# v of the retention stage moved from SyncE's issue queue to ScalarE's

## The chip, the cores and the metric

The kernel runs on one core of one Trainium2 chip. TensorE (PE) does the matrix products, VectorE (DVE) and ScalarE (ACT) the elementwise work, GpSimd (POOL) a little of it, and SyncE (SP) issues transfers. Any of these engines has a queue of instructions that it takes strictly in order; a transfer (DMA) is an instruction in the queue of the engine that issues it, and the data is then moved by 16 DMA engines that all queues share. The metric is device time in microseconds (us), lower is better.

## The reference, cut to what matters

Three parts run one after the other: retention over 8 heads, then two feed-forward layers.

```python
q, k, v: (2 batches, 8 heads, 768 positions, 64), float32; lam: (8,)
for each block of 64 positions:
    intra = (q_b @ k_b.T * Dmask) @ v_b          # Dmask[i, j] = lam ** (i - j) for i >= j
    inter = (q_b * lam ** (pos + 1)) @ kv_state
    out_b = intra + inter
    kv_state = lam ** 64 * kv_state + (k_b * lam ** (63 - pos)).T @ v_b
x = out as (1536 tokens, 512)
h = x @ w_in;  x = (h * tanh(softplus(h))) @ w_out          # layer 1, w_in 512 x 2048
h = x @ w_in2; x = where(h > 0, h, exp(h) - 1) @ w_out2     # layer 2
```

## The kernel before, in words

**Retention** (`retention`, L126) takes the 768 positions of each batch in 6 chunks of 128, 12 chunks in all, numbered 0 to 11, batch by batch in turn. For a chunk it needs three inputs of 256 KB each, called kn, qn and vn by the profile (k3 below is kn of chunk 3, and so on). A loop over rounds n = 0 to 13 (L368) overlaps the chunks. In round n, in this order:

- transfers: k and q of chunk n + 3, v of chunk n + 1, and from round 5 on a weight tile (`raw`, 512 KB, at most two in a round);
- `second_part` of chunk n - 2 on DVE: xl, the low part of x (out of PSUM, minus xh), which frees the single PSUM buffer `o`; the running state `sd`;
- `scores` of chunk n on PE (tile sc, L275), `decay` on DVE (am, L283);
- `transposes` of chunk n + 1 on PE (tile Tp, L231), copied to SBUF by one ACT instruction (tile T, L237). `scores` of the next round reads T;
- `scaled_q` on DVE, `block_state` of chunk n - 2 on ACT (sbd, L350, two instructions);
- `outputs` of chunk n - 1 on PE (o, L305, which reads vn; then st, L314), and `first_part` on ACT: xh, the high part of x (L325);
- `scaled_k` on POOL (kd, L255).

`pin` holds all of these in the order in which they are written. kn, qn and vn have four buffers each (`io`, `bufs=4`), so k of chunk n + 3 is loaded where k of chunk n - 1 was.

All transfers stand in SP's queue, except lam (4 KB), which ACT issues at the start. The framework gives every transfer one of eight completion counters, in turn, in the order in which it plans them; the instruction that issues a transfer first waits until the last holder of its counter has landed, that is, the transfer eight places earlier in that order. The listings of instructions name these counters DMAHW0 to DMAHW7.

**The two layers** follow (`unit`, L518): x is held as a high and a low part (xh, xl) and the weights likewise, so that each product is three matmuls in a fast float32 form. The weights come in 64 tiles of 512 KB which DVE and ACT split (`w_steps`, L86). The first units of layer 1 are interleaved with the end of retention.

Of the kernel before, what the change touches and what calls it, by code (L numbers as in the profile page):

```python
# [18 lines left out]
def kernel(  # L19
# [12 lines left out]
    nc = tc.nc  # L32
# [93 lines left out]
    def retention(beside_load, beside_step, at_end):  # L126
# [12 lines left out]
        def pin(ins):  # L139
            tc.keep_in_program_order(ins)  # L140
            return ins

        def load(n, names, parts=1):
            if not 0 <= n < NC:
                return
            b, c = chunks[n]
            for nm in names:
                nat[n, nm] = io.tile([P, H, D], F32, tag=nm + "n", name=nm + "n")
            for y in range(parts):
                for nm in names:  # L150
                    src, t = {"k": k, "q": q, "v": v}[nm], nat[n, nm]
                    hs = slice(y * H // parts, (y + 1) * H // parts)
                    pin(nc.sync.dma_start(  # L153
                        out=t[:, hs],
                        in_=src[b, hs, c * P:(c + 1) * P, :].rearrange("h p d -> p h d"),
                    ))
# [3 lines left out]
        nc.scalar.dma_start(out=lam_b.rearrange("p h o -> p (h o)"), in_=lam.partition_broadcast(P))  # L160
        load(1, "kq")
        load(2, "kq")
        load(0, "v")

        idle = cst.tile([P, P], F32, name="idle")
        pin(nc.vector.memset(idle, 0.0))
# [5 lines left out]
        def powers(m, end):  # L172
            if m == 1:
                for hh in range(2):
                    rows = slice(hh * D, (hh + 1) * D)
                    pin(nc.vector.tensor_copy(
                        lq[rows, :, 0:1], lam_b[rows].rearrange("p (r t) o -> p r t o", t=2)[:, :, hh]
                    ))
            while m < end:
                pin(nc.vector.tensor_tensor(  # L180
                    out=lq[:, :, m:2 * m], in0=lq[:, :, 0:m],
                    in1=lq[:, :, m - 1:m].to_broadcast([P, PR, m]), op=ALU.mult,
                ))
                m *= 2
# [27 lines left out]
        def warm(count):  # L212
            ps = psO.tile([P, PR, P], F32, tag="o", name="warm")
            for _ in range(count):
                pin(nc.tensor.matmul(ps[:, 0], lhsT=idle, rhs=idle, start=True, stop=True))

        def transposes(n, parts=1):

            T2 = P // 2
            both = wk.tile([P, 2, PR, P], F32, tag="T", name="T")  # L220
            ps = psT.tile([P, 2, 2, PR, T2], F32, tag="T", name="Tp")
            for y in range(parts):
                if y > 0:
                    warm(2)
                rs = slice(y * PR // parts, (y + 1) * PR // parts)
                for z, nm in enumerate(("k", "q")):
                    x = nat[n, nm]
                    for r in range(rs.start, rs.stop):
                        for h in range(2):
                            rows = slice(h * T2, (h + 1) * T2)  # L230
                            pin(nc.tensor.transpose(  # L231
                                ps[:, h, z, r],
                                x[rows, 2 * r:2 * r + 2].rearrange("p h d -> p (h d)"),
                                ident[rows, rows],
                            ))
                if parts == 1:
                    pin(nc.scalar.activation(  # L237
                        out=both.rearrange("p z r (h t) -> p h (z r) t", h=2),
                        in_=ps.rearrange("p h z r t -> p h (z r) t"), func=AF.Copy,
                    ))  # L240
                else:
                    for z in range(2):
                        pin(nc.scalar.activation(
                            out=both[:, z, rs].rearrange("p r (h t) -> p h r t", h=2),
                            in_=ps[:, :, z, rs], func=AF.Copy,
                        ))
            tr[n] = both[:, 0], both[:, 1], ps

        def scaled_k(n):
            if n >= NC:  # L250
                return
            kd = None
            if chunks[n][1] < NCH - 1:
                kd = wk.tile([P, H, D], F32, tag="kd", name="kd", bufs=3)
                pin(nc.gpsimd.tensor_tensor(  # L255
                    out=kd, in0=nat[n, "k"], in1=dm[:, :, P - 1:P].to_broadcast([P, H, D]), op=ALU.mult
                ))
            kds[n] = kd

        def scaled_q(n):  # L260
            if n < NC and chunks[n][1] > 0:
                q2 = wk.tile([P, PR, P], F32, tag="q2", name="q2", bufs=3)
                pin(nc.vector.tensor_tensor(  # L263
                    out=q2.rearrange("p r (h t) -> p h r t", h=2), in0=tr[n][2][:, :, 1],
                    in1=lq.rearrange("p r (h t) -> p h r t", h=2), op=ALU.mult,
                ))
                q2s[n] = q2

        def scores(n):
            kT, qT, _ = tr[n]  # L270
            ps = psS.tile([P, 2, PR, P], F32, tag="sc", name="sc")
            for r in range(PR):
                for hh in range(2):
                    rows = slice(hh * D, (hh + 1) * D)
                    last = pin(nc.tensor.matmul(  # L275
                        ps[:, hh, r], lhsT=kT[rows, r], rhs=qT[rows, r], start=True, stop=True
                    ))
            sc[n] = ps
            return last

        def decay(n):
            a = wk.tile([P, 2, PR, P], F32, tag="am", name="am")
            pin(nc.vector.tensor_tensor(  # L283
                out=a, in0=sc.pop(n), in1=dm.rearrange("p (r t) i -> p t r i", t=2), op=ALU.mult
            ))
            am[n] = a
# [34 lines left out]
        def first_part(n):  # L321
            o, st = done[n]
            b, c = chunks[n]
            t, col = divmod(n * P, TB)
            pin(nc.scalar.activation(out=xh[t][:, :, col:col + P], in_=o, func=AF.Copy))  # L325
            if st is not None and c > 0:
                pin(nc.gpsimd.tensor_tensor(out=sd[b], in0=sd[b], in1=lc, op=ALU.mult))

        def second_part(n):
            o, st = done[n]  # L330
            b, c = chunks[n]
            t, col = divmod(n * P, TB)
            pin(nc.vector.tensor_tensor(  # L333
                out=xl[t][:, :, col:col + P],
                in0=o,
                in1=xh[t][:, :, col:col + P].bitcast(F32),
                op=ALU.subtract,
            ))
            if st is not None:
                if c > 0:  # L340
                    pin(nc.vector.tensor_tensor(out=sd[b], in0=sd[b], in1=st, op=ALU.add))
                else:
                    pin(nc.vector.tensor_copy(sd[b], st))
# [11 lines left out]
        def warm_tiles(count):  # L355

            ps = [psO.tile([P, PR, x], F32, tag=t, name="warm") for t, x in (("o", P), ("st", D))]
            for x in range(count):
                y, z = divmod(x % 4, 2)
                rows, cols = slice(y * D, (y + 1) * D), slice(z * D, (z + 1) * D)  # L360
                pin(nc.tensor.matmul(
                    ps[y][cols, 0, 0:D], lhsT=idle[rows, 0:D], rhs=idle[rows, 0:D], start=True, stop=True
                ))

        warm(7)
        transposes(0, 2)
        warm_tiles(24)
        for n in range(NC + 2):  # L368
            load(n + 3, "kq")
            load(n + 1, "v")  # L370
            beside_load(n, pin)
            if n >= 2:
                second_part(n - 2)
                beside_step(n, 0, pin)
            if n < NC:
                last = scores(n)
                decay(n)
            if n == 1:
                powers(8, P)
            if n + 1 < NC:  # L380
                transposes(n + 1)
            if n == 0:
                warm(2)
                scaled_k(0)
            if n + 1 < NC:
                scaled_q(n + 1)
            if n >= 2:
                block_state(n - 2)
            if 0 < n <= NC:
                outputs(n - 1)  # L390
                first_part(n - 1)
            scaled_k(n + 1)
            beside_step(n, 1, pin)
        with tc.issue_after(last.ins):
# [161 lines left out]
    def beside_load(n, pin):  # L556
        for m in LOAD.get(n, ()):
            pin(w_load(m))

    def beside_step(n, place, pin):  # L560
        for _ in range(STEPS.get((n, place), 0)):
            pin(next(todo))
# [52 lines left out]
```

## Time and profile before

| | |
|---|---|
| median of 3 runs (lowest, highest) | 584.43 us (584.27, 587.32) |
| profiled execution: its own time | 584.7 us |
| profiled execution: span, first to last instruction | 582.4 us |
| PE busy over the span | 574.4 us (99%) |
| DVE, ACT, POOL busy | 430.9, 231.5, 18.9 us |
| granted TensorE clock, mean | 0.999 |
| transfers: kn, qn, vn | 11 each of kn and qn at 256 KB and 4 halves, 12 of vn |
| median issue to landing of vn, kn, qn (256 KB) | 5.2, 5.2, 5.0 us |

The profiled execution's time is 2.3 us longer than its span (start and end of the program lie around it). A row of the timeline gives the start, the length, the engine, the source line and the tiles, and in brackets how long that engine stood idle before it and what ended the idle time. Retention takes about the first 62 us; its last outputs (chunk 11) start at 59.8 us.

### The profile page before, as it was taken

Reading aid. Unit: us, or ns where it says so; the run is one execution under the profiler, and the core shown is the slowest. Engines: PE = TensorE matmul, PEld = TensorE weight load, DVE = VectorE, ACT = ScalarE, POOL = GpSimd, SP = SyncE. Lnnn points to the kernel's source line nnn. Section 1 sums busy time; section 2 is a strip of 40 time slices with the busy share of each in tenths; the row PEclk is TensorE's granted clock in tenths of the full one; section 3 lists DMA queues with packets and bytes.
Section 4 is the critical chain, followed back from the end, with each engine's and each line's share of the span. In section 5 each row is a group of like instructions: output and inputs, shape, how many; then the busy total and the mean of one; then the engine's idle time right before and its main releaser. Section 6 shows DMA issues by size and latency. Waiting matters only on the chain.

```text
span 582.4 us, 8221 instructions
## 1 busy us (share of the span) xinstructions
PE 574.4 (99%) x3282; PEld 481.2 (83%) x3282; DVE 430.9 (74%) x798; ACT 231.5 (40%) x390; POOL 18.9 (3%) x28
## 2 busy tenths in 40 slices
PE   7999999999999999999999999999999999999997
PEld 6988888888888888888888888888888888888886
DVE  5769999998399726993599956995499957944342
ACT  3655554344134124233346445555145235235220
POOL 4430000000000000000000000000000000000000
PEclk9999999999999999999999999999999999999999
DMA  9998333334023301322022221321022310000112
GB/s 172 214 219 233 109 110 108 110 111 142 0 74 108 109 1 37 106 79 69 1 72 73 73 73 36 110 74 71 1 73 72 109 36 1 1 1 0 73 54 92
DMA packets 61030, 46.67 MB, mean 80 GB/s; under 512 B 38848, under 2 KB 55488, under 8 KB 60992
## 3 DMA queue, kind: packets, MB, share of 16 engines
q1 hardware_dynamic: 60848, 46.14, 28.2%
q8 instruction: 26, 0.43, 0.3%
q14 instruction: 12, 0.10, 0.1%
q10 hardware_dynamic: 144, 0.00, 0.0%
HBM read 43.00 MB, written 3.15 MB: 79 GB/s over the span
## 4 chain that ended last, share of the span: by engine, by line
PE 93%; DMA 2%; DVE 2%; SPq 1%; ACT 1%; issue 1%; ACTq 0%
PE h L423 44%; PE y L465 43%; PE o L305 2%; PE y L480 2%; DMA qn<-in_q_dram 1%; DMA vn<-in_v_dram 1%; SPq L153 1%; PE sc L275 1%; PE Tp L231 1%; PE st L314 0%; DVE xl L333 0%; DVE b L104 0%; DVE u L111 0%; DVE q L263 0%; ACT xh L325 0%
## 5 line engine op out<-in xcount | busy, mean ns | idle before, releaser
L423 PE MATMUL h<-xh,w 128*128 128x512 f32 x768 | 240.7, 389 | 0.1
L423 PEld LDWEIGHTS h<-xh,w 128*128 128x128 f32 x768 | 144.1, 188 | 30.5 <-ACT w L118 0.6
L423 PE MATMUL h<-xl,w 128*128 128x512 f32 x384 | 149.4, 389 | 0.0
L465 PE MATMUL y<-w,g 128*128 128x512 f32 (+1 forms) x588 | 132.5, 385 | 0.0
L465 PEld LDWEIGHTS y<-w,g 128*128 128x128 f32 x588 | 108.9, 188 | 22.1
L465 PE MATMUL y<-g,w 128*128 128x512 f32 x528 | 121.5, 389 | 0.0
L465 PEld LDWEIGHTS y<-g,w 128*128 128x128 f32 x528 | 99.1, 188 | 20.6
L493 DVE TENSOR_TENSOR acc<-acc,y 128x512 f32<-128x512 f32 (+1 forms) x73 | 49.4, 677 | 58.6 <-PE y L465 58.6
L433 DVE TENSOR_TENSOR g<-g,g 128x512 fp32r<-128x512 f32 x96 | 65.9, 687 | 30.0 <-ACT g L432 27.5
L423 PEld LDWEIGHTS h<-xl,w 128*128 128x128 f32 x384 | 72.1, 188 | 14.9
L118 ACT ACTIVATE w<-m 128x512 fp32r<-128x512 f32 x64 | 40.2, 628 | 102.0 <-PE h L423 55.2
L432 ACT ACTIVATE g<-g 128x512 fp32r<-128x512 f32 x96 | 60.2, 628 | 16.3 <-DVE g L450 14.8
L119 DVE TENSOR_TENSOR w<-m,w 128x512 fp32r<-128x512 f32 x64 | 43.9, 686 | 24.4 <-ACT w L118 23.7
L441 ACT ACTIVATE g<-h 128x512 f32<-128x512 f32 x48 | 28.5, 596 | 71.1 <-PE h L423 71.1
L447 ACT ACTIVATE e<-h 128x512 f32<-128x512 f32 x48 | 28.6, 596 | 59.0 <-PE h L423 58.0
L450 DVE SCALAR_TENSOR_TENSOR g<-e,h 128x512 f32<-128x512 f32 x48 | 32.8, 683 | 17.1 <-ACT e L448 17.0
L104 DVE SCALAR_TENSOR_TENSOR b<-raw,b 128x512 int32<-128x512 int32 x64 | 44.1, 690 | 0.4
L111 DVE SCALAR_TENSOR_TENSOR u<-raw,u 128x512 f32<-128x512 uint32 x64 | 43.7, 684 | 0.2
L116 DVE TENSOR_TENSOR m<-b,u 128x512 f32<-128x512 f32 x64 | 43.7, 684 | 0.1
L448 ACT ACTIVATE e<-e 128x512 f32<-128x512 f32 x48 | 30.3, 631 | 1.1
L98 DVE TENSOR_SCALAR m<-m 128x512 f32<-128x512 f32 x64 | 27.1, 424 | 0.1
L107 DVE TENSOR_SCALAR u<-b 128x512 int32<-128x512 int32 x64 | 26.8, 420 | 0.4
(52 smaller groups left out, 304.3 us busy)
## 6 DMA issues: line engine op xcount, KB each, us to landing
raw<-in_moe_w_in_dram SPq DMA_DIRECT2D x32, 512.0 KB, 3.7
raw<-in_moe_w_out_dram SPq DMA_DIRECT2D x32, 512.0 KB, 3.3
vn<-in_v_dram SPq DMA_DIRECT2D x12, 256.0 KB, 5.2
kn<-in_k_dram SPq DMA_DIRECT2D x11, 256.0 KB, 5.2
qn<-in_q_dram SPq DMA_DIRECT2D x11, 256.0 KB, 5.0
out_dram<-acc SPq DMA_DIRECT2D x11, 256.0 KB, 2.0
kn<-in_k_dram SPq DMA_DIRECT2D x2, 128.0 KB, 3.5
qn<-in_q_dram SPq DMA_DIRECT2D x2, 128.0 KB, 3.6
```

Source lines behind the costliest of these rows:

```text
L104: yield nc.vector.scalar_tensor_tensor(out=b, in0=hw, scalar=-0x40000000, in1=b, op0=ALU.bitwise_and, op1=ALU.bitwise_or)
L111: yield nc.vector.scalar_tensor_tensor(out=uf, in0=lw, scalar=2.0 ** -52, in1=uf, op0=ALU.mult, op1=ALU.mult)
L116: yield nc.vector.tensor_tensor(out=mf, in0=bf, in1=uf, op=ALU.add)
L118: nc.scalar.activation(out=w[:, 0], in_=mf, func=AF.Copy)
L119: yield nc.vector.tensor_tensor(out=w[:, 1], in0=mf, in1=w[:, 0].bitcast(F32), op=ALU.subtract)
L423: nc.tensor.matmul(h, lhsT=lt, rhs=rt, start=(kk == 0 and n == 0), stop=(kk == KD - 1 and n == 2),)
L432: nc.scalar.activation(out=gg[:, 0], in_=g, func=AF.Copy)
L433: nc.vector.tensor_tensor(out=gg[:, 1], in0=g, in1=gg[:, 0].bitcast(F32), op=ALU.subtract)
L448: nc.scalar.activation(out=e, in_=e, func=AF.Exp, scale=-1.0)
L450: nc.vector.scalar_tensor_tensor(out=g, in0=e, scalar=-1.0, in1=h, op0=ALU.add, op1=ALU.max)
L465: nc.tensor.matmul(y, lhsT=lt, rhs=rt, start=(i == 0 and n == 0), stop=(i == G - 1 and n == 2),)
L493: nc.vector.tensor_tensor(out=dst, in0=dst, in1=y, op=ALU.add)
```

## The change

v of every chunk is issued by ACT instead of SP, and at another place in the round: v0 behind the copies of the transposes of chunk 0, v1 in round 0 behind the copy of the transposes of chunk 1, and v of chunk n + 2 at the end of round n, behind xh of chunk n - 1. Nothing is computed otherwise.

```diff
-                    pin(nc.sync.dma_start(
+                    pin((nc.scalar if nm == "v" else nc.sync).dma_start(
...
         load(1, "kq")
         load(2, "kq")
-        load(0, "v")
...
         transposes(0, 2)
+        load(0, "v")
         warm_tiles(24)
         for n in range(NC + 2):
             load(n + 3, "kq")
-            load(n + 1, "v")
...
             if n == 0:
+                load(1, "v")
                 warm(2)
                 scaled_k(0)
...
                 outputs(n - 1)
                 first_part(n - 1)
+            load(n + 2, "v")
             scaled_k(n + 1)
```

On PE, DVE and POOL the instructions stand as before. ACT's queue in the middle of retention, before: the copy T of chunk 7, sbd of chunk 4, xh of chunk 5, the copy T of chunk 8.

```order
L237 ACTIVATE T<-Tp 128x2x8x64 [waits PE_49,Activation_49]
L350 ACTIVATE sbd_139<-sd_137 64x4x64 [waits DVE_49,Activation_49]
L350 ACTIVATE sbd_139<-sd_137 64x4x64 [waits Activation_49]
L325 ACTIVATE xh_65<-o 128x4x128 [waits PE_49]
L237 ACTIVATE T<-Tp 128x2x8x64 [waits PE_49,Activation_49]
```

The same stretch of ACT's queue in the changed kernel:

```order
L236 ACTIVATE T<-Tp 128x2x8x64 [waits PE_49,Activation_49]
L349 ACTIVATE sbd_137<-sd_135 64x4x64 [waits DVE_49,Activation_49]
L349 ACTIVATE sbd_137<-sd_135 64x4x64 [waits Activation_49]
L324 ACTIVATE xh_65<-o 128x4x128 [waits PE_49]
L153 DMA vn<-in_v_dram 128x8x64 [waits DMAHW7_49]
L236 ACTIVATE T<-Tp 128x2x8x64 [waits PE_49,Activation_49]
```

Between xh of chunk 5 and the copy T of chunk 8 the issue of v8 now stands, with a wait for counter 7. SP's queue before, from the first weight tile on: raw0, k9, q9, v7, k10, q10, v8, k11.

```order
L75 DMA raw<-in_moe_w_in_dram 128x4x256 [waits DMAHW4_49]
L153 DMA kn<-in_k_dram 128x8x64 [waits DMAHW5_49,PE_49,Pool_49]
L153 DMA qn<-in_q_dram 128x8x64 [waits DMAHW6_49,PE_49]
L153 DMA vn<-in_v_dram 128x8x64 [waits DMAHW7_49,PE_49]
L153 DMA kn<-in_k_dram 128x8x64 [waits DMAHW0_49,PE_49,Pool_49]
L153 DMA qn<-in_q_dram 128x8x64 [waits DMAHW1_49,PE_49]
L153 DMA vn<-in_v_dram 128x8x64 [waits DMAHW2_49,PE_49]
L153 DMA kn<-in_k_dram 128x8x64 [waits DMAHW3_49,PE_49,Pool_49]
```

SP's queue in the changed kernel from the same weight tile on: raw0, k9, q9, k10, q10, k11, q11, raw1.

```order
L75 DMA raw<-in_moe_w_in_dram 128x4x256 [waits DMAHW2_49]
L153 DMA kn<-in_k_dram 128x8x64 [waits DMAHW4_49,PE_49,Pool_49]
L153 DMA qn<-in_q_dram 128x8x64 [waits DMAHW7_49,DMAHW5_49,PE_49]
L153 DMA kn<-in_k_dram 128x8x64 [waits DMAHW7_49,PE_49,Pool_49]
L153 DMA qn<-in_q_dram 128x8x64 [waits DMAHW3_49,DMAHW0_49,PE_49]
L153 DMA kn<-in_k_dram 128x8x64 [waits DMAHW2_49,PE_49,Pool_49]
L153 DMA qn<-in_q_dram 128x8x64 [waits DMAHW6_49,DMAHW3_49,PE_49]
L75 DMA raw<-in_moe_w_in_dram 128x4x256 [waits DMAHW4_49]
```

The v's are gone from it. The counters of both queues together are dealt in this order in the changed kernel (the planner places a v among SP's transfers by when it expects ACT to come to it; a and b are the halves of chunk 0):

```
counter   0    1    2     3    4    5    6    7
         lam  k0a  q0a   k0b  q0b  k1   q1   k2
         q2   k3   q3    v0   k4   q4   k5   q5
         v1   v2   k6    q6   v3   k7   q7   v4
         k8   q8   raw0  v5   k9   q9   v6   k10
         q10  v7   k11   q11  raw1 raw2 raw3 v8
         v9   v10  v11
```

Each transfer waits for the one above it: v1 for q2, v2 for k3, v3 for k4, v4 for q5, v8 for k10.

## Rows read from the trace of the kernel before

**Rows 1.** Busy time by engine: retention and rest (us, count; PEclk, DMA share, GB/s)

```profile
0.00:62.00 62.00, 57.26 (x991) 52.66 (x991) 47.51 (x79) 31.41 (x53) 18.89 (x28) 1.00 0.92 201
62.00:582.40 520.40, 517.17 (x2292) 428.54 (x2292) 383.36 (x720) 200.06 (x338) 0.00 (x0) 1.00 0.21 66
sum 582.40, PE 574.43 PEld 481.19 DVE 430.87 ACT 231.48 POOL 18.89; mean PE 287.21 PEld 240.60 DVE 215.44 ACT 115.74 POOL 9.44
```

**Rows 2.** Waits of PE in 0 to 62 us (us in total, times, longest)

```profile
PE o L305 <- DMA vn<-in_v_dram: 1.5, 1, 1.5
PE Tp L231 <- DMA qn<-in_q_dram: 1.2, 2, 1.0
...
PE sc L275 <- ACT T L237: 0.5, 1, 0.5
```

**Rows 3.** Busy time in three stretches of 2 us; last columns DMA share, GB/s

```profile
8.00:10.00 2.00, 1.52 (x28) 1.27 (x26) 1.23 (x1) 1.02 (x1) 1.96 (x2) 1.00 1.32 224
...
12.00:14.00 2.00, 0.94 (x18) 0.97 (x20) 1.79 (x6) 0.72 (x1) 0.00 (x0) 1.00 0.71 159
14.00:16.00 2.00, 2.00 (x52) 1.93 (x47) 1.49 (x4) 0.60 (x1) 1.06 (x1) 1.00 1.11 239
```

**Rows 4.** Timeline of SP's queue: issue of q9, v7, k10 (start, length)

```profile
33.52 0.89 SPq L153 DMA_DIRECT2D qn<-in_q_dram  x1
34.50 2.33 SPq L153 DMA_DIRECT2D vn<-in_v_dram  x1
36.94 1.62 SPq L153 DMA_DIRECT2D kn<-in_k_dram  x1
```

**Rows 5.** Issues starting at 2.89, 5.67, 6.75, 17.05, 36.94: last column us to landing

```profile
kn<-in_k_dram SPq DMA_DIRECT2D x1, 256.0 KB, 4.2
...
qn<-in_q_dram SPq DMA_DIRECT2D x1, 256.0 KB, 5.0
...
vn<-in_v_dram SPq DMA_DIRECT2D x1, 256.0 KB, 6.2
...
qn<-in_q_dram SPq DMA_DIRECT2D x1, 256.0 KB, 6.0
...
kn<-in_k_dram SPq DMA_DIRECT2D x1, 256.0 KB, 5.3
```

**Rows 6.** Timeline of ACT: its one transfer, then the round of xh of chunk 5

```profile
0.74 0.43 ACTq L160 DMA_DIRECT2D lam_b<-in_lam_dram  x1
1.20 1.28 ACT L168 ACT_TABLE_LOAD   x1 [1.20 <-PEq L597]
...
33.49 0.60 ACT L325 ACTIVATE xh<-o 128x512 fp32r<-128x512 f32 x1
35.53 1.03 ACT L237 ACTIVATE T<-Tp 128x1024 f32<-128x1024 f32 x1 [1.45 <-PE Tp L231]
36.58 0.86 ACT L350 ACTIVATE sbd<-sd 64x256 f32<-64x256 f32 x2
```

**Rows 7.** Tile vn: issues, duration ns min/median/max, first and last start

```profile
L153 SPq DMA_DIRECT2D vn<-in_v_dram x12: 467/1060/2629, 6.8 to 47.8; - x12
```

**Rows 8.** Timeline of PE: scores of chunks 4, 7, 8, 9 and what stands between

```profile
21.82 1.16 PE L275 MATMUL sc<-T 64*128 64x128 f32 x16
...
33.77 1.16 PE L275 MATMUL sc<-T 64*128 64x128 f32 x16
...
35.36 1.09 PE L305 MATMUL o<-q,sbd 128*64 128x128 f32 x16
...
37.72 1.16 PE L275 MATMUL sc<-T 64*128 64x128 f32 x16
...
40.14 0.47 PE L231 MATMUL Tp<-ident,qn 64*128 64x64 f32 x8 [1.02 <-DMA qn<-in_q_dram]
...
42.90 1.16 PE L275 MATMUL sc<-T 64*128 64x128 f32 x16
```

**Rows 9.** Timeline of DVE: xl of chunk 5

```profile
34.12 0.69 DVE L333 TENSOR_TENSOR xl<-o,xh 128x512 fp32r<-128x512 f32 x1 [0.81 <-ACT xh L325]
```

## The prediction

> **What bounds the kernel now.** I read the busy times by stretch first. Outside retention PE is busy 517.17 of 520.40 us [rows 1]: nothing can be gained there, and a delay of PE in retention is passed on to the end one for one. In the first 62 us PE is busy 57.26 us [rows 1]; of the idle 4.7 us the table of waits puts 1.5 on one transfer of v, 1.2 on q, and 0.5 on ACT's copy T [rows 2]. The two waits for data, 2.7 us together, are the most that the change can win: 0.46% of 584.7 us.
>
> Next comes the transfer side. The DMA share of retention is 0.92 at 201 GB/s, against 0.21 after it [rows 1]. Where the queue is full the share stands over 1 (it counts packets, and these overlap) at 224 GB/s [rows 3]. k1 was issued at 2.89 and landed 4.2 us later, at 7.09; q2, three transfers on, was issued at 5.67 and landed 5.0 later, at 10.67 [rows 5]: 3.58 / 3 = 1.19 us for each 256 KB. A round of PE without a wait takes 37.72 - 33.77 = 3.95 us [rows 8] and wants three of them, 3.58 us, and 512 KB of weights in some rounds. So transfers and PE run nearly level in this stage, and SP issues without a pause: q9, v7 and k10 stand end to end [rows 4]. The stream has holes too: 159 GB/s at share 0.71 around the late landing of v0 [rows 3], which came 6.2 us after 6.75, at 12.95, 2.28 behind q2 instead of 1.19 [rows 5].
>
> **The change part by part.** Twelve issues leave SP and twelve enter ACT. On SP one issue of vn takes 1.06 us in the median, 0.47 to 2.63 [rows 7]. ACT's only transfer so far took 0.43 us for 4 KB, and the next ACT instruction starts only behind it, at 1.20 [rows 6]; so an issue keeps ACT's queue from going on. For 256 KB on ACT I take 1.06, the nearest row, with 0.43 and 2.63 as its ends.
>
> In a round of the middle this issue alone would be hidden. xh of chunk 5 ends at 34.09, the copy T of chunk 8 begins at 35.53 after 1.45 us of waiting for PE [rows 6]: 1.06 fits with 0.4 to spare. Behind it there is a little more cover: T is followed by sbd (0.86) and xh (0.60) [rows 6], and xl must be done before PE's next outputs can write the single buffer o. xl of chunk 5 ended at 34.81 [rows 9] and those outputs began at 35.36 [rows 8]: 0.55 us. Beyond about 0.9 us of delay (0.4 + 0.55) PE stands.
>
> What is not hidden is the wait in front of the issue. Each transfer waits until the one eight places earlier in the planner's order has landed. While SP issued everything, such a wait held only other transfers. Now it holds ACT, and behind v in ACT's queue stands the copy T that PE's scores need; SP's queue itself only loses entries, so k and q come to the DMA engines earlier and the v's share with them. The total is unchanged: k10 is in both kernels preceded by k, q of chunks 0 to 9, v0 to v7 and raw0.
>
> - v1 waits for q2 and v2 for k3, both in front of the copy T of chunk 2. k3 lands no sooner than v0 did (it takes its place in SP's queue, and v0 now runs beside it), 12.95. The win at v0 is spent here: seven transfers still have to land before the outputs of chunk 0.
> - v4 waits for q5. Before, q5 landed at 17.05 + 6.0 = 23.05 [rows 5], when fifteen loads of 256 KB had gone; that holds T of chunk 4 until 23.05 + 1.06 and sets scores of chunk 4 at 23.05 + 1.06 + 1.03 = 25.1 instead of 21.82 [rows 8], 3.3 us late.
> - v5 to v7 wait for q6 to q8. ACT is then late already, and these have landed about when it gets there.
> - v8 waits for k10, and this wait sets the sum, the earlier ones lie inside it. Before, k10 landed at 36.94 + 5.3 = 42.24 [rows 5]. If the same loads take the same time, T of chunk 8 begins at 42.24 + 1.06 = 43.3 and scores of chunk 8 at 43.3 + 1.03 = 44.3 instead of 37.72. Before, 42.90 - 37.72 = 5.18 us passed to the scores of chunk 9, with the wait of 1.02 for q9 in it [rows 8]. That wait goes, since q9 is ahead of k10; the round is 3.95, plus about 0.6 because xl follows T by 0.86 + 0.60 + 0.69 and is late for the buffer o. Scores of chunk 9 come at 48.9 instead of 42.90: +6.0.
> - If instead the holes are filled by the second queue, k10 lands at 10.67 plus 23 loads of 1.19 and raw0 at twice that, 40.4: +4.2 by the same steps.
> - Behind v8, v9 to v11 wait for q10, v7 and k11, which the pause has let through. SP's weight tiles get no later. PE has no slack to make the loss good.
>
> Between 6.0 and 4.2 I take 5.0, about the middle, since I see no reason why a second queue should fill all holes or none. The profiled execution's 584.7 becomes 589.7; the median of the runs shown lies 0.27 below that execution, so I forecast 589.4 us.
>
> The Trainium skill, "DMA: Bandwidth & Descriptors", section "Rules for kernel authors", says that spreading transfers over several issuing engines brings no bandwidth, because all run on the same 16 DMA engines, and saves issue time only. By it the first figure, +6.0, would stand. The trace agrees as far as it goes: at 8 to 10 us one queue has the DMA share at 1.32 [rows 3]; that two queues move no more, no run here shows.
>
> **The rivals.**
>
> *The transfers get faster with two queues, and the waits fall away (not slower).* For it: SP's queue is packed, and single stretches reach 239 GB/s [rows 3], 1.10 us for 256 KB. Then k10 lands at 10.67 + 25 x 1.10 = 38.2, T of chunk 8 at 39.3, scores of chunk 8 at 40.3 and of chunk 9 at 44.8: +1.9, 586.3, which is no measurable change. For ACT to find k10 landed when it comes to v8, at about 35.2 (34.09 and one issue that was not hidden), a load must take (35.2 - 10.67) / 25 = 0.98 us, 267 GB/s; from there on both waits for data go and the kernel gains up to 2.7: 581.7. Against it: 1.19 us held over three loads in a row with issues waiting.
>
> The Trainium skill's page "Perfetto Trace Analysis", section "DMA Optimizations", speaks for this rival: where descriptor generation is the bottleneck, with the issuing engine's track solid, balancing transfers over several engines may help. SP's track is solid here [rows 4], but the share of 1.32 says that the DMA engines are as well.
>
> *An issue on ACT is much longer than on SP's median (slower still).* SP's worst is 2.63 [rows 7]; two queues that issue at once may slow each other. ACT's round would be 1.03 + 0.86 + 0.60 + 2.63 = 5.1 against 3.95. That costs 1.6 at v8 and 1.2 in each of the three rounds with an issue behind it, 5.2 on top of 5.0: 594.9. Against it: 1.06 is the median with the queue full.
>
> *Only the early waits bind.* If SP, freed of v, gets k10 through by some 37, the loss is what v2 and v4 leave less the waits for data: 3.3 - 2.7 = 0.6, 585.3. Against it: k10 cannot pass k9 and q9 in the queue, and the total in front of it is fixed by 1.19 us a load.
>
> **How the numbers follow.** What a measurement of this kernel can tell from no change is about 0.5%, 2.9 us. The forecast (v8 waits for k10, +3.5 to +7) has 0.62, with its own range 587.9 to 591.4; the longer issue 0.12; early waits only 0.09; faster transfers 0.17, of which 0.13 within 0.5% and 0.04 beyond (a gain of over 2.9 exceeds what the waits hold, so this needs something that I don't see). Of the forecast 0.03 falls within 0.5%. So faster 0.04, same 0.13 + 0.09 + 0.03 = 0.25, slower 0.59 + 0.12 = 0.71. The range: 584.3 at the low end, which leaves out the part of the faster transfers that gains anything (0.1), and 593.5 at the high end, which takes in a longer issue of up to 2 us (0.07 left out).
>
> **What would show it.** In the changed profile: vn issued by ACT with about 1 us each; ACT idle in front of several of them, most in front of v4 and v8; T of chunk 8 starting about 1 us behind the landing of k10, at 41.5 to 43.3; PE waiting for ACT's T at the scores of chunks 2 to 4 and 8, and no more for v at the outputs of chunk 0 or q at chunk 9; scores of chunk 9 near 47.9; beyond 62 us PE as busy as before. I am wrong if k10 lands before 37 (the transfers got faster), if ACT does not stand in front of v8, or if the issue on ACT takes 2 us.

## The result, and the profile after

The changed kernel takes 588.51 us in the median of 8 runs (588.21 to 589.22) against 584.43 us before (583.56 to 587.32, 8 runs). The ratio is 1.0066, 95% interval 1.005 to 1.0081 (ratios, here and below, are taken over all runs and are not the quotient of the two medians): slower by 4.1 us by the medians, forecast were 5.0. The profiled execution took 588.91 us, with a span of 586.7 us against 582.4 before.

Busy time by stretch shows first that the loss lies in retention. The columns are those of [rows 1].

```profile
0.00:66.00 66.00, 59.23 (x990) 54.48 (x990) 47.21 (x78) 31.14 (x52) 18.82 (x28) 0.97 0.95 188
66.00:586.70 520.70, 517.28 (x2292) 428.61 (x2292) 383.49 (x720) 200.26 (x339) 0.00 (x0) 1.00 0.21 66
```

The same 2292 matmuls as in the second row of [rows 1] fill the last 520.7 us, PE busy 517.28 (517.17 before). They only start some 4 us later. What PE waited for until then (compare [rows 2]):

```profile
PE sc L274 <- ACT T L236: 4.4, 4, 2.4
PE o L304 <- DVE xl L332: 1.3, 3, 0.6
PE warm L214 <- DVE idle L165: 1.1, 1, 1.1
```

The waits for v and q, 2.7 us, are gone; ACT's copy T has risen from 0.5 to 4.4 us, and xl from 0.2 to 1.3. The row for xl before, which [rows 2] leave out:

```profile
PE o L305 <- DVE xl L333: 0.2, 1, 0.2
```

ACT's timeline shows the copy held behind issues of v (a row marked ACTq is an issue; x2 runs from the first of two to the end of the second):

```profile
11.28 3.45 ACTq L153 DMA_DIRECT2D vn<-in_v_dram  x2
14.84 1.02 ACT L236 ACTIVATE T<-Tp 128x1024 f32<-128x1024 f32 x1 [4.61 <-DMA kn<-in_k_dram]
...
20.20 0.60 ACT L324 ACTIVATE xh<-o 128x512 fp32r<-128x512 f32 x1
23.81 0.37 ACTq L153 DMA_DIRECT2D vn<-in_v_dram  x1
24.29 1.02 ACT L236 ACTIVATE T<-Tp 128x1024 f32<-128x1024 f32 x1 [3.49 <-DMA qn<-in_q_dram]
...
33.62 0.37 ACTq L153 DMA_DIRECT2D vn<-in_v_dram  x1
33.64 0.60 ACT L324 ACTIVATE xh<-o 128x512 fp32r<-128x512 f32 x1
...
37.59 0.60 ACT L324 ACTIVATE xh<-o 128x512 fp32r<-128x512 f32 x1
40.94 0.37 ACTq L153 DMA_DIRECT2D vn<-in_v_dram  x1
41.41 1.02 ACT L236 ACTIVATE T<-Tp 128x1024 f32<-128x1024 f32 x1 [3.23 <-PE o L304]
```

Landing of k3 (issued at 6.62), q5 (15.41) and k10 (32.48), last column:

```profile
kn<-in_k_dram SPq DMA_DIRECT2D x1, 256.0 KB, 7.7
...
qn<-in_q_dram SPq DMA_DIRECT2D x1, 256.0 KB, 8.3
...
kn<-in_k_dram SPq DMA_DIRECT2D x1, 256.0 KB, 8.4
```

That is 14.32, 23.71 and 40.88. v2's issue ends at 14.73, v4 is issued at 23.81, v8 at 40.94: each as its counter's last holder lands (v8 3.35 us after ACT began xh of chunk 5, 2.75 after it ended). For the last wait the profile names PE's outputs as releaser. T does not read these; it reads the transposes, of which the last ended at 39.51 (39.09 + 0.42, below). And T begins 0.10 to 0.11 us behind the end of each of the three held issues (14.73 to 14.84, 24.18 to 24.29, 41.31 to 41.41), so it was the transfer that v8 waited for. PE's timeline has the answer to each hold (compare [rows 8]):

```profile
11.91 1.09 PE L304 MATMUL o<-am,vn 128*64 128x128 f32 x16
...
15.91 1.55 PE L274 MATMUL sc<-T 64*128 64x128 f32 x16 [2.45 <-ACT T L236]
...
20.54 1.16 PE L274 MATMUL sc<-T 64*128 64x128 f32 x16
...
25.37 1.16 PE L274 MATMUL sc<-T 64*128 64x128 f32 x16 [0.80 <-ACT T L236]
...
27.59 1.09 PE L304 MATMUL o<-q,sbd 128*64 128x128 f32 x16 [0.57 <-DVE xl L332]
...
37.85 1.16 PE L274 MATMUL sc<-T 64*128 64x128 f32 x16
...
39.09 0.42 PE L230 MATMUL Tp<-ident,qn 64*128 64x64 f32 x8
...
42.49 1.16 PE L274 MATMUL sc<-T 64*128 64x128 f32 x16 [0.62 <-ACT T L236]
...
44.72 1.09 PE L304 MATMUL o<-q,sbd 128*64 128x128 f32 x16 [0.57 <-DVE xl L332]
...
47.08 1.16 PE L274 MATMUL sc<-T 64*128 64x128 f32 x16
```

PE before, at the outputs of chunk 0 and the scores of chunks 2 and 3:

```profile
13.06 1.09 PE L305 MATMUL o<-am,vn 128*64 128x128 f32 x16 [1.46 <-DMA vn<-in_v_dram]
...
14.55 1.16 PE L275 MATMUL sc<-T 64*128 64x128 f32 x16
...
17.73 1.16 PE L275 MATMUL sc<-T 64*128 64x128 f32 x16
```

The outputs of chunk 0 start 1.15 us earlier than before and need not wait for v0, but the scores of chunk 2 come at 15.91 instead of 14.55, those of chunk 4 at 25.37 instead of 21.82, of chunk 7 at 37.85 instead of 33.77, of chunk 9 at 47.08 instead of 42.90: +4.18.

One row of the loss was not in the prediction. After the idle 2.45 us PE's granted clock was at its lower level (0.50, 1.2 GHz) from about 16.5 to 20 us; the last three columns are clock, DMA share and GB/s:

```profile
16.00:18.00 2.00, 2.00 (x31) 2.00 (x32) 2.00 (x4) 0.35 (x1) 0.00 (x0) 0.63 1.32 218
18.00:20.00 2.00, 2.00 (x24) 1.88 (x24) 1.26 (x2) 1.56 (x3) 0.00 (x0) 0.51 1.33 218
```

PE's own account adds up: waits for T +3.9, for xl +1.1, for data -2.7, the round of chunk 2 at the lower clock +1.45 (4.63 us to the scores of chunk 3, 3.18 before), a start 0.35 later (scores of chunk 0 at 7.51, 7.16 before): 4.1 us. This adds up what PE did; whether the lower clock cost anything is for the fourth experiment.

### The profile page after: what moved, and what is told of

It is laid out like the page before. It is cut to its first block, busy times and chain, and to the rows that moved or that the text cites. A ratio compares the mean times of both kernels' runs of the same rounds, so it can differ in the third digit from the quotient of the medians.

```text
span 586.7 us, 8219 instructions
## 1 busy us (share of the span) xinstructions
PE 576.5 (98%) x3282; PEld 483.1 (82%) x3282; DVE 430.7 (73%) x798; ACT 231.4 (39%) x390; POOL 18.8 (3%) x28
## 4 chain that ended last, share of the span: by engine, by line
PE 92%; DVE 2%; DMA 2%; ACT 1%; SPq 1%; issue 1%; ACTq 0%
PE h L424 44%; PE y L466 43%; PE o L304 2%; PE y L481 2%; DMA kn<-in_k_dram 1%; PE sc L274 1%; SPq L153 1%; DMA qn<-in_q_dram 1%; ACT T L236 1%; PE Tp L230 0%; DVE xl L332 0%; PE st L313 0%; DVE b L104 0%; ACT xh L324 0%; DVE u L111 0%
## 5 line engine op out<-in xcount | busy, mean ns | idle before, releaser
L100 DVE TENSOR_SCALAR b<-m 128x512 int32<-128x512 int32 x64 | 26.8, 421 | 0.3
```

## The experiments

The theory: ACT is held in front of a v until the transfer eight places earlier has landed, and T with it. The rivals: v, asked for earlier and on a queue of its own, takes transfer time from k and q, which PE needs sooner; or PE's lower clock is part of the loss.

**Older holders.** Three buffers for k and q keep SP from running far ahead, so that each v waits for an older transfer.

```diff
-nat[n, nm] = io.tile([P, H, D], F32, tag=nm + "n", name=nm + "n")
+nat[n, nm] = io.tile([P, H, D], F32, tag=nm + "n", name=nm + "n", bufs=4 if nm == "v" else 3)
```

> The changed kernel with three buffers instead of four for k and q (v keeps four). SP can then run less far ahead, and the transfer eight places before a v becomes an older one: v1 waits for q1 instead of q2, v2 for k2 instead of k3, v4 for q4 instead of q5, v8 for q8 instead of k10. Theory (ACT is held in front of v until that transfer lands, and with it the copy T): the idle time of ACT in front of v4 and v8 goes, scores of chunk 4 start near 22 instead of 25.4, scores of chunk 9 near 43 instead of 47.1, total 584 to 585.5 us. Rival (v asked for earlier takes transfer time from k and q, ACT's hold is not what costs): 588 to 589 us, PE then waits for k or q.

Measured: 585.82 us against 584.26 for the kernel before beside it, ratio 1.0026 (1.0016 to 1.0036). The holds at v4 and v8 are gone, as expected (scores of chunk 4 at 23.17, of chunk 8 at 38.97), but the total lies above the range of the theory, by 0.3 us. In this program v9 is the one that waits for k10. ACT's timeline, then PE's:

```profile
38.71 0.60 ACT L324 ACTIVATE xh<-o 128x512 fp32r<-128x512 f32 x1
42.12 0.38 ACTq L153 DMA_DIRECT2D vn<-in_v_dram  x1
42.60 1.02 ACT L236 ACTIVATE T<-Tp 128x1024 f32<-128x1024 f32 x1 [3.30 <-PE o L304]
```

```profile
43.68 1.16 PE L274 MATMUL sc<-T 64*128 64x128 f32 x16 [0.69 <-ACT T L236]
...
46.14 1.09 PE L304 MATMUL o<-q,sbd 128*64 128x128 f32 x16 [0.81 <-DVE xl L332]
```

k10 was issued at 33.43 and landed 8.7 us later, at 42.13; v9 left at 42.12. The hold moved with its holder.

**The order alone.** The loads stand as in the changed kernel, all on SP.

```diff
-pin((nc.scalar if nm == "v" else nc.sync).dma_start(
+pin(nc.sync.dma_start(
```

> The loads written in the order of the changed kernel, all of them issued by SP. Theory: the counters hold only SP, ACT is free, 584 to 585.5 us, as before. Rival (the order in which v is asked for costs, whoever issues it): 587 us or more.

Measured: 585.89 us against 584.26, ratio 1.0029 (1.0018 to 1.0039), between the two. Without ACT's holds most of the loss is gone, but not all. The trace doesn't say cleanly where the rest is: PE's waits are no longer than before (0.65 us for q9), and the first scores start at 8.25 instead of 7.16, since the early matmuls ran slowly for longer (scores of chunk 0 in 2.08 us instead of 1.16, while the column for the granted clock shows 1.00); that start differs between profiles of other kernels too (6.88 to 8.45). Of this late start of 2 us (scores of chunk 1 at 11.97, 9.94 before) 0.65 is left at the scores of chunk 9 (43.55, 42.90 before). With one queue the new order does not hold up k3 and q3: they landed at 13.93 and 15.00 (14.00 and 14.96 before). What the 1.6 us consist of stays open.

**v4 and v8 given back.**

```diff
-pin((nc.scalar if nm == "v" else nc.sync).dma_start(
+pin((nc.scalar if nm == "v" and n not in (4, 8) else nc.sync).dma_start(
...
+if n in (3, 7):  load(n + 1, "v")      # behind k and q of the round
...
-load(n + 2, "v")
+if n not in (2, 6):  load(n + 2, "v")
```

> The changed kernel with v4 and v8 alone given back to SP, behind k and q of their round as before. Theory: the holds in front of the copy T of chunks 4 and 8 go; the hold of v2 for k3 stays (scores of chunk 2 near 15.9). What PE lost at chunks 4 and 8 in the changed kernel is 0.80 + 0.57 + 0.62 + 0.57 = 2.6 us; part of it comes back as waits for k or q, so 586 to 587.3 us. Rival (something else than ACT's holds): 588.5 us as it is.

Measured: 586.17 us against 584.26, ratio 1.0034 (1.0021 to 1.0047), within the range. The hold of v2 for k3 stays (PE idle 2.57 us before the scores of chunk 2), the scores of chunk 4 come at 24.51 without a wait, and v9 now has the late hold (issued at 43.18, q10 landed at 43.12; PE lost 0.36 + 0.81 us).

**The clock.** Five idle matmuls fill the gap in front of the scores of chunk 2.

```diff
+if n == 2:
+    ws = psS.tile([P, 2, PR, P], F32, tag="sc", name="sc")
+    for _ in range(5):
+        pin(nc.tensor.matmul(ws[:, 0, 0], lhsT=idle, rhs=idle, start=True, stop=True))
```

> The changed kernel with five idle matmuls on PE in front of the scores of chunk 2, where PE stood idle for 2.45 us and the granted clock was 0.50 for some 3 us afterwards. Theory (the hold of ACT until q5 lands decides when the scores of chunk 4 start): the clock stays at 1.00, scores of chunk 3 start about 1.4 us earlier (19.1 instead of 20.5), scores of chunk 4 stay at 25.4, total 588 to 589 us. Rival (the lower clock is part of the loss): 587.1 us.

Measured: 588.48 us, as the changed kernel. The clock stayed up:

```profile
16.00:18.00 2.00, 1.85 (x33) 1.69 (x33) 1.50 (x4) 0.00 (x0) 0.60 (x1) 1.00 1.34 217
```

```profile
25.32 1.16 PE L274 MATMUL sc<-T 64*128 64x128 f32 x16 [1.15 <-ACT T L236]
```

The round of chunk 2 took 3.08 us (16.71 to 19.79) instead of 4.63, though it began 0.8 us later in this execution, and the scores of chunk 4 start at 25.32, where they did (25.37): what the clock gives back, the hold of v4 takes as a longer wait (1.15 instead of 0.80). The eight runs of the changed kernel say the same: the five with a mean clock of 0.997 took 588.21 to 588.91 us, the three with 0.999 or 1.000, which had little or nothing of the dip, 588.5 to 589.22. The lower clock costs nothing here.

**Control for the three buffers.** The same line as in the first experiment, in the kernel before.

> The kernel before (all loads on SP) with three buffers instead of four for k and q: the control for the first experiment, which has the same buffers with v on ACT and came out 1.6 us above before. Theory (SP is paced by the transfers, not by free buffers, and the 1.6 us come from ACT's hold in front of v9): 584.0 to 584.9 us. Rival (three buffers cost by themselves): 585.5 us or more.

Measured: 584.45 us against 584.49, ratio 1.0 (0.9992 to 1.0009). The buffers cost nothing.

**No hold left.** Three buffers, and v9 to v11 given back as well.

```diff
-pin((nc.scalar if nm == "v" else nc.sync).dma_start(
+pin((nc.scalar if nm == "v" and n < 9 else nc.sync).dma_start(
...
+if n >= 8:  load(n + 1, "v")           # behind k and q of the round
...
-load(n + 2, "v")
+if n < 7:  load(n + 2, "v")
```

> The first experiment with v9, v10 and v11 given back to SP; v0 to v8 stay on ACT. There ACT issued v9 at 42.12, as k10 landed at 42.13, and PE lost 0.69 + 0.81 = 1.5 us behind it. Theory: that hold goes, ACT is never held for long, 584.0 to 585.0 us. Rival (what is left over before lies at the start, or in v's share of the transfers): 585.5 us or more.

Measured: 585.71 us against 584.49, ratio 1.0032 (1.002 to 1.0044): the rival's range. ACT no longer stops PE (0.47 us, as before), and still 1.2 us remain by the medians, 1.9 by the ratio. PE's timeline shows new waits:

```profile
15.61 0.47 PE L230 MATMUL Tp<-ident,kn 64*128 64x64 f32 x8 [0.82 <-DMA kn<-in_k_dram]
...
17.64 0.46 PE L230 MATMUL Tp<-ident,qn 64*128 64x64 f32 x8 [1.56 <-DMA qn<-in_q_dram]
```

q3, issued at 9.61, landed at 17.61 (14.96 before). v1, issued by ACT at 8.76, ahead of it, landed at 14.26, though PE wants v1 only behind k3 and q3. The control has the same buffers and SP asks for q3 at the same time (9.60), with v1 behind it (10.26). The landing of q3, in the control and here:

```profile
qn<-in_q_dram SPq DMA_DIRECT2D x1, 256.0 KB, 5.5
...
qn<-in_q_dram SPq DMA_DIRECT2D x1, 256.0 KB, 8.0
```

PE's waits for data in the control:

```profile
PE o L305 <- DMA vn<-in_v_dram: 1.3, 1, 1.3
...
PE Tp L231 <- DMA qn<-in_q_dram: 0.5, 1, 0.5
```

These are 1.8 us; here they are 2.9 (2.1 for q, 0.8 for k), 1.1 more. So the first rival holds too: a second queue lets v go ahead of k and q that are needed sooner. The hold at v9 that is gone gained only 0.1 us over the first experiment, where PE lost 1.5 to it; the two profiled executions started differently (scores of chunk 0 at 8.34 there, 7.06 here), and their waits can't be taken one from the other.

**v later onto ACT.** v0 to v2 on SP as before, v3 to v8 on ACT, v9 to v11 on SP, three buffers.

```diff
-pin(nc.sync.dma_start(
+pin((nc.scalar if nm == "v" and 3 <= n <= 8 else nc.sync).dma_start(
...
-load(n + 1, "v")
+if not 3 <= n + 1 <= 8:  load(n + 1, "v")
...
+if 3 <= n + 2 <= 8:  load(n + 2, "v")  # behind first_part
```

> Three buffers for k and q; v0 to v2 on SP at their place of before, v3 to v8 on ACT at the place of the changed kernel, v9 to v11 on SP. Theory (two losses: ACT's holds, gone here as in the sixth experiment, and v1 and v2 in ACT's queue going ahead of k3 and q3, which made PE wait 0.82 + 1.56 us for them there): both are gone, scores of chunk 3 start near 17.7 instead of 19.5, total 584.0 to 584.8 us. Rival (any v on a second queue takes transfer time from k and q): 585.3 us or more, with waits of PE for k or q later.

Measured: 586.03 us against 584.73, ratio 1.0019 (1.001 to 1.0028): again the rival. The waits of chunk 3 are gone (scores at 18.13), and others stand one and two chunks later, for q4 and q5:

```profile
20.14 0.46 PE L231 MATMUL Tp<-ident,qn 64*128 64x64 f32 x8 [0.61 <-DMA qn<-in_q_dram]
...
25.55 0.46 PE L231 MATMUL Tp<-ident,qn 64*128 64x64 f32 x8 [0.74 <-DMA qn<-in_q_dram]
```

q4 was issued at 13.67 and v3 at 14.11, by ACT; v3 landed first, at 19.11, q4 at 20.07, though v3 is wanted a round later. PE's waits for data sum to 3.4 us in this profile, 1.8 in the control.

**v0 alone on ACT**, in the kernel before, and the same with three buffers.

```diff
-pin(nc.sync.dma_start(
+pin((nc.scalar if nm == "v" and n == 0 else nc.sync).dma_start(
...
-load(0, "v")
 transposes(0, 2)
+load(0, "v")
```

> The kernel before with v0 alone issued by ACT, behind the copies T of chunk 0. Theory: v0 lands near 11.8 instead of 12.95 and waits for nothing, PE's outputs of chunk 0 start about 1.1 us earlier, scores of chunk 2 near 13.4; q3 and later q9 then bind, so that the gain is lost again: 583.9 to 584.6 us. Rival (the early gain stays): 583.3 us.

> The same with three buffers for k and q, where PE waited 0.45 us for q9 instead of 1.02. Theory: 583.8 to 584.6 us. Rival (the early gain stays): 583.2 us.

Measured: 584.77 us (ratio 1.0003, 0.9994 to 1.0011) and 585.13 us (1.0007, 0.9998 to 1.0016) against 584.73: no change, but not by the way I expected. v0 landed at 12.87 (12.95 before), and q2 fell back from 10.67 to 12.45 beside it:

```profile
12.45 0.46 PE L230 MATMUL Tp<-ident,qn 64*128 64x64 f32 x8 [1.36 <-DMA qn<-in_q_dram]
```

PE waits 1.36 us for q2 where it waited 1.46 for v0. Seven loads have to land, and here it makes no odds which comes last.

**raw0 later**, in the kernel before (rounds 7 and 6), and round 7 with the split of **No hold left**.

```diff
-LOAD = {5: (0,), 8: (1,), ...
+LOAD = {7: (0,), 8: (1,), ...          # then {6: (0,), ...
```

> The kernel before with the first weight tile (raw0) loaded in round 7 instead of round 5, so that k9, q9, k10 and q10 go ahead of it. Theory (transfers and PE run level, so that a load moved behind q9 removes PE's wait of 1.02 us for q9): 583.0 to 583.8 us. Rival (the wait moves on to a later k, q or v, or DVE waits for raw0): 584.3 us.

> Both: three buffers for k and q, v0 to v8 on ACT, v9 to v11 on SP, raw0 in round 7. Theory: neither a hold of ACT nor the wait for q9 is left, and v0 lands earlier than before: 582.5 to 583.8 us, the best of all. Rival (splitting the queues gives nothing once the holds are gone): equal to the kernel before with raw0 in round 7.

> The kernel before with raw0 loaded in round 6 instead of round 5 (the seventh experiment, which used round 7, held DVE's queue until raw0 landed at 45.81 with xl behind it). Theory: k9 and q9 now go ahead of raw0 and PE's wait of 1.02 us for q9 goes; raw0 lands near 41, before DVE asks for it at 42.4: 583.0 to 583.9 us, faster than either kernel. Rival (the wait moves on to k10, q10 or v8, or DVE still waits for raw0): 584.3 us or more.

Measured: 588.51 us in round 7 (ratio 1.0073, 1.0057 to 1.0089), 585.98 us with the split (1.0024, 1.0013 to 1.0035), 584.49 us in round 6 (1.0, 0.9988 to 1.0013). With the split, raw0 landed at 43.44, in time, and PE waited 1.49 us for q3 instead, so that neither figure that I had written came out. In round 7 alone raw0 landed at 45.81, and DVE, whose queue had its first weight step in front of xl, stood for 4.72 us:

```profile
45.88 0.43 DVE L94 TENSOR_SCALAR m<-raw 128x512 int32<-128x512 int32 x1 [4.72 <-DMA raw<-in_moe_w_in_dram]
...
46.68 0.68 DVE L333 TENSOR_TENSOR xl<-o,xh 128x512 fp32r<-128x512 f32 x1
```

This is the same trap on another engine: a wait for a transfer in an in-order queue, with the next step of PE behind it (PE waited 4.16 us for that xl, and its granted clock was 0.50 from 46 to 52 us, so that the loss is not the wait alone). My rival had named this wait and priced it at nothing, 584.3 us. In round 6 the profile shows the wait for q9 gone, span 581.5 us, but over 12 runs the median differs by 0.36 us, inside the interval; the gain that I expected did not come, though the waits that my rival named did not either. No version tried beats the kernel before by more than its measurement can tell.

## Why the prediction was right

**The step that set the sum held.** T of chunk 8 was held until k10 landed and began 0.53 us behind it. Two sizes in that step were off, both the same way. The issue on ACT took 0.37 us, not 1.06, below the lower end of 0.43 that I had for it. It holds what stands behind it, as T shows, but not what stands in front: v7, behind xh of chunk 4 in the queue, was issued at 33.62, and that xh began at 33.64. And k10 landed at 40.88, where the middle of my two figures, 42.24 and 40.4, was 41.3. The middle was a guess between two reasoned figures; the landing lies nearer to the lower one, with most holes filled, and that it missed by only 0.4 is luck. T of chunk 8 came at 41.41 against 42.4, and from its scores to those of chunk 9 it took 4.59 us against 4.55 by my steps: +4.18 at chunk 9 instead of +5.0. That this hold alone sets the sum, with the earlier ones inside it, is read from the landing of k10; no run has v8's hold without those of v2 and v4.

**The early holds** came where they were put: v2 behind k3, v4 behind q5, with the scores of chunk 4 3.55 us late against 3.3. That this is so close is in part luck: q5 landed at 23.71, 0.66 later than the row of before that I took, and the issue was 0.69 shorter than I took it. I expected ACT to stand longest in front of v4 and v8; it stood longest at v2 (idle 4.61 us, PE 2.45), since k3 landed at 14.32, where I had reckoned with 12.95. So the early gain at v0 was more than spent: the scores of chunk 2 came 1.36 us late. In the experiments with v0 alone it was spent too, though there q2 took its place.

**A second queue brought no faster transfers.** The rule of the Trainium skill that I weighed ("DMA: Bandwidth & Descriptors", "Rules for kernel authors") agrees with the trace: with both queues at work 16 to 20 us shows 218 GB/s at share 1.32 to 1.33, where one queue had 224 at 1.32 [rows 3]. The +6.0 that I hung on it does not follow from it, since one queue had not kept the engines full. What k10 gained, 1.36 us against before, fits with filled holes: 12 to 14 us has 222 GB/s instead of 159 [rows 3], and 20 to 22, before and after:

```profile
20.00:22.00 2.00, 2.00 (x46) 1.93 (x42) 1.47 (x2) 1.86 (x4) 0.54 (x1) 1.00 0.70 132
...
20.00:22.00 2.00, 2.00 (x51) 1.93 (x48) 1.33 (x4) 0.77 (x2) 1.64 (x2) 1.00 1.37 223
```

**What the sum did not contain:** v going ahead of k and q. I wrote that the total in front of k10 is unchanged, which is right for k10, and missed that inside the total the order matters for k3, q3, q4 and q5. **No hold left** and **v later onto ACT**, with hardly a hold left, still lose 1.2 and 1.3 us. In the changed kernel v2 and v4 wait for just such late transfers, k3 and q5. Taking 1.2 or 1.3 from 4.1 leaves 2.8 to 2.9 us for the holds, an estimate: by the ratios it is 2.0 to 2.8, that the two parts simply add was not shown, and the 1.6 us that the new order loses on one queue are not explained.

**The rivals.** Faster transfers: refuted. A longer issue on ACT: refuted, it is shorter. Early waits only: not so, v8 is there, but it adds less than the sum made it seem. The price that I gave this rival, 3.3 - 2.7 = 0.6, was wrong: the 21.82 against which the 3.3 is measured has the wait for v0 in it already, so that only the 1.02 for q9 could still come off, which leaves about 2.3. In the changed kernel PE was 4.08 us late at the scores of chunk 7, ahead of v8's hold; less 1.02 that is about 3.1, to which v8 added some 1.1 (an estimate from these rows).

## What to carry to other kernels

In this case a transfer issued from a compute engine's queue brought its waits along. Before moving one, find what its issue waits for in the new order (a shared completion counter, a free buffer) and what stands behind it in that queue. Transfers and compute ran level here; the second queue filled holes but added no speed where the engines were full, and it lost what the single queue had kept, that data arrive in the order in which they are needed.

## What the runs showed of the hardware that was not expected

PE's granted clock fell to 0.50 after one idle stretch of 2.45 us (16.5 to 20 us in the changed kernel), while the kernel before kept 1.00 through one of 1.46 us. The length of the last gap does not tell the two apart: the clock also fell behind the 1.49 us for q3 in the run with the split and raw0 in round 7 (0.50 from 18 to 20 us), and stayed at 1.00 behind the 1.56 us for q3 in **No hold left**. An issue of 256 KB on ACT took 0.37 us in the median, where SP took 1.06 for the same tile [rows 7]; with ACT issuing too, SP's median went from 0.92 to 1.15 us for kn and from 1.03 to 1.59 for qn. SP can be as quick: k3, asked for after a pause of SP's queue in **No hold left**, took 0.37 us (at 9.13). What makes SP's issues long was not tried.
